# Interleaving the dense work of a 512-token chunk, in pieces of up to four matmuls, with the attention forward of the next chunk

## The chip, the cores and the metric

The kernel runs on one core of one Trainium2 chip. The metric is device microseconds (us) from the first to the last instruction of that core, as a median of several runs. PE is the matmul engine, DVE the vector engine, ACT the scalar engine (which computes the exponentials here and also issues 8 DMAs in the kernel before), POOL the GpSimd engine, SP the engine that issues most DMAs here (1161 of 1266 in the kernel before). "PE clock" is the granted clock of PE as a share of full speed, as the profile records it.

## The reference

It is one transformer block with adaptive layer norm, forward and backward: S = 2048 tokens, D = 512, 32 heads of 16, an MLP 512 → 1792 → 512 with squared ReLU, all in bf16. The kernel returns the output and nine gradients. Cut to what matters:

```python
def block(x, wqkv, wo, w1, b1, w2, b2, c, w_mod):
    sa, ca, ga, sb, cb, gb = split(silu(c) @ w_mod, 6)
    h = layernorm(x) * (1 + ca) + sa
    x = x + ga * (attention(h, wqkv, heads=32) @ wo)       # softmax attention
    h = layernorm(x) * (1 + cb) + sb
    r = relu(h @ w1 + b1)
    return x + gb * (r * r @ w2 + b2)

def reference(inputs, grad_out):
    out, vjp = jax.vjp(block, *inputs)
    return out, *vjp(grad_out)
```

## The kernel before

It runs in stages, one after the other: preparation (layer norm, Q, K, V), attention forward, the dense stage (projection, MLP forward and MLP backward, for each of four 512-token chunks), the weight gradients of the dense layers, the attention backward, and the rest. The first two of the following pieces are what the change weaves together.

The attention forward is a loop over units. A unit is one 128-key tile against 512 queries for a group of four heads. It has four score matmuls, two exponentials of 128x1024 elements on ACT, and, two units later, four PV matmuls. All of these matmuls use only a quarter of the array each (32 rows or 32 columns, placed by `tile_position`; the trace names them 32\*128 and 128\*32, and the dense ones 128\*128).

```python
psS = pool("psS", bufs=3, PSUM)     # score tiles of two banks each
psO = pool("psO", bufs=2, PSUM)     # accumulators of PV
# ... cut: fload brings the K and Q tiles of a group of heads ...
def fscore(u):
    ET = ework.tile([P, 4, 512], BF, name="ET")
    for pair in range(2):
        ps = psS.tile([P, 2, 512], F32, name="psST")
        for hi in range(2):
            r = 32 * (2 * pair + hi)
            PE.matmul(ps[:, hi, :], kt_sb[r:r + 32, kt * P:(kt + 1) * P], qt_sb[r:r + 32, :],
                      start=True, stop=True, tile_position=(r, 0))
        ACT.activation(ET[:, 2 * pair:2 * pair + 2, :], ps[:], AF.Exp, scale=SCALE)
# ... cut: fpv: four PV matmuls into oacc; after 16 key tiles oacc is evicted ...

# build of the padded, transposed QKV weights for the last stage, beside the forward:
for t3 in range(3):
    for hg in range(HG):
        # ... cut: every second hg loads a transposed tile tmpT ...
        for hq in range(4):
            POOL.dma_start(out=wT_bld[o0:o0 + DH, ...], in_=tmpT[r0:r0 + DH, :])   # 96 in all
POOL.dma_start(out=wT_st[:], in_=wT_bld[:])

for u in range(NF + 6):             # NF = 512 units
    if u < NF: fscore(u)
    if 2 <= u < NF + 2: fpv(u - 2)
    if fdone ...: ffinish(...)      # normalise a finished chunk, store it in o_st
```

Only then comes the dense stage, with all weights resident in both orientations and seven PSUM banks:

```python
psm = pool("psM", bufs=7, PSUM)
def dense_chunk(c):
    # ... cut: loads; a = O @ wo, layer norm, then ...
    for fc in range(FC):                                  # 14 blocks of the MLP
        pz = mm()                                         # one PSUM bank
        for ic in range(DC):                              # four matmuls 128x128x512
            PE.matmul(pz[:], w1_nat[:, ic, fc * P:(fc + 1) * P], h2T[:, ic, :], ...)
        # ... eviction with ReLU on ACT or DVE; square on DVE ...
    # ... cut: r*r @ w2, the same two products backward, dOs = da @ wo^T ...
for c in range(QC):
    for _ in dense_chunk(c): pass
```

The weight-gradient stage loads activations and gradients back from DRAM (gf_g, O_g, da_g, h_g and the tokens of the MLP, 22 MB in all; the first ten loads, 19 MB, are issued before any result is written) and runs 544 matmuls (the trace has records of 538) into eight banks of PSUM, with evictions alternating between ACT and DVE:

```python
for key, src in (("gf", gf_st), ("O", o_st), ("da", da_st), ("h2", h2_st)):
    SP.dma_start(out=toks[key][:], in_=src[:])
# ... cut: loads of s and dz ...
for oc in range(DC):
    acc = psg.tile([P, 512], F32, name="aw")              # bufs=8
    for t in range(TT): PE.matmul(acc[:], toks["O"][...], toks["da"][...], ...)
    if oc % 2 == 0: ACT.activation(wblk, acc, AF.Identity)
    else:           DVE.tensor_copy(wblk, acc)
# ... cut: the same for the gradients of w2 and w1 ...
```

Of the kernel before, what the change touches and what calls it, by code (L numbers as in the profile page):

```python
# [17 lines left out]
BF = dt.bfloat16  # L18
# [16 lines left out]
def kernel(  # L35
# [46 lines left out]
    dOs_tok = persist.tile([P, TT, D], BF, name="dOs_tok")  # L82
# [7 lines left out]
    o_st = dram.tile([P, TT, D], BF, name="o_st")  # L90
    da_st = dram.tile([P, TT, D], BF, name="da_st")
# [188 lines left out]
    with ExitStack() as ph:  # L280
        wk = ph.enter_context(tc.tile_pool(name="phC", bufs=2))
        ework = ph.enter_context(tc.tile_pool(name="phCe", bufs=4))
        psS = ph.enter_context(tc.tile_pool(name="psS", bufs=3, space=bass.MemoryType.PSUM))
        psO = ph.enter_context(tc.tile_pool(name="psO", bufs=2, space=bass.MemoryType.PSUM))
# [3 lines left out]
        fh, fe, fcur = {}, {}, {}  # L288
# [8 lines left out]
        def fscore(u):  # L297
            qc, hg, kt = funits[u]
            qt_sb, kt_sb = fh[qc, hg]
            ET = ework.tile([P, 4, 512], BF, name="ET", tag="ET")  # L300
            fe[u] = ET
            for pair in range(2):
                ps = psS.tile([P, 2, 512], F32, name="psST", tag="psST")
                for hi in range(2):
                    r = 32 * (2 * pair + hi)
                    PE.matmul(ps[:, hi, :], kt_sb[r:r + 32, kt * P:(kt + 1) * P], qt_sb[r:r + 32, :],  # L306
                              start=True, stop=True, tile_position=(r, 0))
                ACT.activation(ET[:, 2 * pair:2 * pair + 2, :], ps[:], AF.Exp, scale=SCALE)  # L308

        def fpv(u):  # L310
            qc, hg, kt = funits[u]
            if kt == 0:
                fcur["o"] = psO.tile([P, 512], F32, name="oacc", tag="oacc")
                if hg == 0:
                    fcur["rr"] = wk.tile([H, 512], F32, name="rrows", tag="rrows")
                    fcur["ou"] = wk.tile([P, 4, HG, P], BF, name="O_un", tag="O_un")
# [19 lines left out]
        fdone = []  # L336

        def ffinish(qc, rr, ou):
            O_c = wk.tile([P, 4, D], BF, name="O_c", tag="O_c")
            for ti in range(4):  # L340
                t = qc * 4 + ti
                pr = psO.tile([P, 512], F32, name="prinv", tag="oacc")
# [6 lines left out]
            SP.dma_start(out=o_st[:, qc * 4:(qc + 1) * 4, :], in_=O_c[:])  # L349

        NF = len(funits)
        fload(0, 0)
        wtp = ph.enter_context(tc.tile_pool(name="phW", bufs=1))
        wT_bld = wtp.tile([P, 16, D], BF, name="wT_bld")
        POOL.memset(wT_bld[:], 0.0)
        for t3 in range(3):
            for hg in range(HG):
                if hg % 2 == 0:
                    tmpT = wtp.tile([P, D], BF, name="tmpT", tag="tmpT", bufs=2)
                    SP.dma_start(out=tmpT[:], in_=A_wqkv[:, (t3 * 4 + hg // 2) * P:(t3 * 4 + hg // 2 + 1) * P], transpose=True)  # L360
                for hq in range(4):
                    r0 = (hg % 2) * 64 + hq * DH
                    o0 = 32 * hq + (DH if t3 == 1 else 0)
                    POOL.dma_start(out=wT_bld[o0:o0 + DH, (0 if t3 == 0 else 8) + hg, :], in_=tmpT[r0:r0 + DH, :])
        POOL.dma_start(out=wT_st[:], in_=wT_bld[:])
        with tc.manual_schedule(engines={PE.engine, ACT.engine}):
            for u in range(NF + 6):
                if u < NF:
                    if funits[u][2] == 4 and u + TT < NF:
                        fload(*funits[u + TT][0:2])  # L370
                    fscore(u)
                if 2 <= u < NF + 2:
                    fpv(u - 2)
                if fdone and (u - 2 >= fdone[0][0] or u == NF + 5):
                    ffinish(*fdone.pop(0)[1:])

    vaugpool.release()



    with ExitStack() as ph:
        ffw = ph.enter_context(tc.tile_pool(name="ffw", bufs=1))
        wk = ph.enter_context(tc.tile_pool(name="phM", bufs=2))
        cb = ph.enter_context(tc.tile_pool(name="phMc", bufs=1))
        psm = ph.enter_context(tc.tile_pool(name="psM", bufs=7, space=bass.MemoryType.PSUM))
        psr = ph.enter_context(tc.tile_pool(name="psMr", bufs=1, space=bass.MemoryType.PSUM))
        wo_nat = ffw.tile([P, DC, D], BF, name="wo_nat")
        SP.dma_start(out=wo_nat[:], in_=A_wo.rearrange("(oc p) j -> p oc j", p=P))
        w1_nat = ffw.tile([P, DC, FF], BF, name="w1_nat")
        SP.dma_start(out=w1_nat[:], in_=B_w1.rearrange("(ic p) f -> p ic f", p=P))  # L390
        w2_nat = ffw.tile([P, FC, D], BF, name="w2_nat")
        SP.dma_start(out=w2_nat[:], in_=B_w2.rearrange("(fc p) d -> p fc d", p=P))
        b2row = ffw.tile([1, D], BF, name="b2row")
        SP.dma_start(out=b2row[:], in_=B_b2.rearrange("(o f) -> o f", o=1))
        w1T = ffw.tile([P, FC, D], BF, name="w1T")
        w2T = ffw.tile([P, DC, FF], BF, name="w2T")
        woT = ffw.tile([P, DC, D], BF, name="woT")
        for oc in range(DC):
            SP.dma_start(out=w2T[:, oc, :], in_=B_w2[:, oc * P:(oc + 1) * P], transpose=True)
        for fc in range(FC):  # L400
            SP.dma_start(out=w1T[:, fc, :], in_=B_w1[:, fc * P:(fc + 1) * P], transpose=True)
        for oc in range(DC):
            SP.dma_start(out=woT[:, oc, :], in_=A_wo[:, oc * P:(oc + 1) * P], transpose=True)
        prow = psr.tile([P, 512], F32, name="prow")

        def rowsum(j, src, t):
            PE.matmul(prow[32 * j:32 * j + 1, :], ones_bf[:, 0:1], src, start=(t == 0), stop=(t == TT - 1),
                      tile_position=(0, 32 * j), skip_group_check=True)

        def mm():  # L410
            return psm.tile([P, 512], F32, name="pm", tag="pm")

        def t4():
            return cb.tile([P, 4, DC, P], BF, name="T4", tag="T4", bufs=2)

        def flat(x):
            return x.rearrange("p a b -> p (a b)")

        def dense_chunk(c):
            ts = slice(4 * c, 4 * c + 4)  # L420
            O_c = cb.tile([P, 4, D], BF, name="O_m", tag="O_m")
            SP.dma_start(out=O_c[:], in_=o_st[:, ts, :])
            x0_c = cb.tile([P, 4, D], BF, name="x0_c", tag="x0_c")
            SP.dma_start(out=x0_c[:], in_=x_dram[:, ts, :])
            g_c = cb.tile([P, 4, D], BF, name="g_c", tag="g_c")
            SP.dma_start(out=g_c[:], in_=g_dram[:, ts, :])
            OT = t4()
            SP.dma_start(out=OT.rearrange("p t o q -> p (t o) q"), in_=flat(O_c), transpose=True)
            gf_c = cb.tile([P, 4, D], BF, name="gf_c", tag="gf_c")
            DVE.tensor_tensor(gf_c[:], g_c[:], gb_bc.unsqueeze(1).to_broadcast([P, 4, D]), ALU.mult)  # L430
            SP.dma_start(out=gf_st[:, ts, :], in_=gf_c[:])
            gfT = cb.tile([P, 4, DC, P], BF, name="gfT", tag="gfT")
            SP.dma_start(out=gfT.rearrange("p t o q -> p (t o) q"), in_=flat(gf_c), transpose=True)
            x1_c = cb.tile([P, 4, D], BF, name="x1_c", tag="x1_c")
            a_c = cb.tile([P, 4, D], BF, name="a_c", tag="a_c")
            xn2_c = cb.tile([P, 4, D], BF, name="xn2_c", tag="xn2_c")
            mv4 = wk.tile([P, 4, 2], F32, name="mv4", tag="mv4")
            for ti in range(4):
                pa = mm()
                for oc in range(DC):  # L440
                    PE.matmul(pa[:], OT[:, ti, oc, :], wo_nat[:, oc, :], start=(oc == 0), stop=(oc == DC - 1))  # L441
                ACT.activation(a_c[:, ti, :], pa[:], AF.Identity)  # L442
                tmp = wk.tile([P, D], BF, name="atmp", tag="atmp")
                DVE.tensor_tensor(tmp[:], a_c[:, ti, :], ga_bc, ALU.mult)
                DVE.tensor_tensor(x1_c[:, ti, :], tmp[:], x0_c[:, ti, :], ALU.add)
                st6 = wk.tile([P, 6], F32, name="st6", tag="st6")
                DVE.bn_stats(st6[:], x1_c[:, ti, :])
                DVE.bn_aggr(mv4[:, ti, :], st6[:])
            sd4 = wk.tile([P, 4], F32, name="sd4", tag="sd4")
            DVE.tensor_scalar(sd4[:], mv4[:, :, 1], EPS, None, ALU.add)  # L450
            ACT.activation(sd4[:], sd4[:], AF.Sqrt)
            DVE.reciprocal(rstd2[:, ts], sd4[:])
            for ti in range(4):
                t = 4 * c + ti
                DVE.tensor_scalar(xn2_c[:, ti, :], x1_c[:, ti, :], mv4[:, ti, 0:1], rstd2[:, t:t + 1], ALU.subtract, ALU.mult)
# [527 lines left out]
```

## Time and profile before

The time is 3627.5 us (median of four fast runs, 3620.1 to 3629.0); the profiled execution spans 3621.8 us. The stages, from windows of the trace:

| stage | from – to, us | length | what limits it |
|---|---|---|---|
| preparation | 0 – 287 | 287 | PE and DVE |
| attention forward | 287 – 1236 | 949 | ACT, 940 us busy |
| dense stage | 1236 – 1727 | 491 | nothing is full: PE 276 us busy, DVE 253 |
| weight gradients | 1727 – 1858 | 131 | PE, 113 us |
| start of backward | 1858 – 1871 | 13 | DMA |
| attention backward | 1871 – 3307 | 1436 | PE, DVE and ACT together |
| rest | 3307 – 3622 | 315 | not touched |

The head of the page, its busy line, and three rows of the picture of 40 slices (each digit is a slice of 90.5 us; 9 means busy for 90% or more; PEclk is the clock in tenths):

```profile
span 3621.8 us, 47309 instructions
...
PE 2861.2 (79%) x17554; PEld 811.5 (22%) x17605; DVE 1861.7 (51%) x2725; ACT 2166.0 (60%) x3501; POOL 338.4 (9%) x390
...
PE   3688999999999665556778888888888888886746
...
ACT  0008999999999600000037777878777877784202
...
PEclk7985555555555577778888887888878878897967
```

The row of ACT is full (9) from slice 5 to slice 13 and then falls to 0: that is the forward followed by the dense stage. PE shows 9 in the same slices, but its clock is 5 there, half speed. The two stages need different engines and stand one after the other: this is what the change wants to use.

The windows view of the kernel before gives the same by stage. Its columns are the stretch and its length, then busy time and number of instructions of PE, PE weight loads, DVE, ACT and POOL, then the clock, the share of the DMA engines and GB/s:

```profile
core 0: us, PE busy (x) PEld busy (x) DVE busy (x) ACT busy (x) POOL busy (x), PEclk, DMA share, GB/s
287.00:1236.00 949.00, 870.28 (x4108) 163.69 (x4108) 33.42 (x56) 940.37 (x1025) 64.33 (x126) 0.50 0.12 34
1236.00:1727.00 491.00, 275.93 (x1089) 107.17 (x1108) 253.40 (x590) 30.90 (x49) 88.13 (x101) 0.76 0.62 147
1727.00:1858.00 131.00, 112.68 (x538) 53.74 (x544) 10.10 (x17) 9.65 (x17) 0.50 (x1) 0.92 0.51 205
1858.00:1871.00 13.00, 0.15 (x3) 0.14 (x4) 2.58 (x2) 1.35 (x2) 3.04 (x2) 0.62 0.98 348
1871.00:3307.00 1436.00, 1243.17 (x10224) 340.84 (x10220) 1188.81 (x1024) 1119.97 (x2206) 142.37 (x103) 0.84 1.15 204
```

The group of the exponentials, with busy time, mean length in ns, and the idle time of ACT just before them and what ended most of it:

```profile
L308 ACT ACTIVATE ET<-psST 128x1024 bf16<-128x1024 f32 x1024 | 939.1, 1697 | 5.9 <-PE psST L306 5.9
```

ACT was idle for only 5.9 us before 1024 exponentials: ACT sets the pace of the forward, 0.917 us for each, 1.83 us for a unit. A unit in the timeline (start, length, engine, operation; `x4` joins four matmuls):

```profile
801.82 0.62 PE L322 MATMUL oacc<-ET,vaug 128*32 128x512 bf16 x4
...
802.37 1.35 PE L306 MATMUL psST<-qt_sb,kt_sb 32*128 32x512 bf16 x4
...
803.65 0.62 PE L322 MATMUL oacc<-ET,vaug 128*32 128x512 bf16 x4
```

Four score matmuls are spread over 1.35 us and four PV matmuls over 0.62 us, so that PE counts as busy for nearly the whole of 1.83 us. But it streams only about 3 x 0.427 = 1.28 us of that (an estimate: the four PV matmuls start within 0.01 us of each other and the four score matmuls in two pairs, 0.74 us apart, which I count as three streams; 427 ns is the spacing that matmuls of this width have at half clock in the first burst of the dense stage, 1301.9 to 1304.5 us).

### The profile page before, as it was taken

The page shows a single profiled execution, that of the slowest core. Times are in us where ns is not written, and L with a number is a line of the kernel's source. Part 1 is how long each engine was busy: PE and PEld are TensorE (multiplying, and loading weights), DVE is VectorE, ACT ScalarE, POOL GpSimd, SP SyncE. Part 2 cuts the span into 40 slices and gives each one's busy share as a digit, 9 for nine tenths or more (in the row PEclk, how much of TensorE's full clock was granted, in tenths as well). Part 3 has the DMA queues.
Part 4 walks back from the last instruction along what each step waited for, and adds up shares of the span by engine and source line. Part 5 has one row for each costly group of instructions (what it writes and reads, how often), then busy time and mean ns, then how long its engine had stood idle before and what let it go on. Part 6 is the DMA issues. An engine that isn't in the chain of part 4 may idle for free.

```text
span 3621.8 us, 47309 instructions
## 1 busy us (share of the span) xinstructions
PE 2861.2 (79%) x17554; PEld 811.5 (22%) x17605; DVE 1861.7 (51%) x2725; ACT 2166.0 (60%) x3501; POOL 338.4 (9%) x390
## 2 busy tenths in 40 slices
PE   3688999999999665556778888888888888886746
PEld 1231111111111122222332222222222222221312
DVE  8860000000000145555038787888788878884781
ACT  0008999999999600000037777878777877784202
POOL 2006000000000012121000101010101010000000
PEclk7985555555555577778888887888878878897967
DMA  3123010010011355566669999999999999999112
GB/s 122 60 112 108 27 33 27 27 33 27 27 33 33 95 142 141 137 159 116 264 166 199 211 200 212 200 212 200 210 199 214 195 214 197 205 198 207 64 64 88
DMA packets 1331989, 487.18 MB, mean 135 GB/s; under 512 B 1275299, under 2 KB 1307559, under 8 KB 1328557
## 3 DMA queue, kind: packets, MB, share of 16 engines
q1 hardware_dynamic: 1312030, 478.38, 63.0%
q10 hardware_dynamic: 16512, 2.10, 0.4%
q0 software_dynamic: 3216, 3.68, 0.4%
q8 instruction: 139, 2.28, 0.2%
q14 instruction: 92, 0.75, 0.1%
HBM read 101.28 MB, written 71.98 MB: 48 GB/s over the span
## 4 chain that ended last, share of the span: by engine, by line
PE 24%; DMA 17%; DVE 5%; ACT 5%; issue 3%; SPq 1%; POOL 0%; DVEq 0%; POOLq 0%; ACTq 0%
DMA dsT<-dS_u 14%; PE psS_u L686 6%; PE dqacc L738 4%; ACT E_u L688 4%; PE accVK L723 3%; PE accVK L714 2%; PE psS_x L686 2%; DVE dS_u L700 2%; PE aw L619 1%; SPq L910 1%; PE aw L628 1%; DVE dqkv_tok L814 1%; PE psD_u L698 1%; DVE dh1acc L822 1%; DMA iqs<-q_st 1%
## 5 line engine op out<-in xcount | busy, mean ns | idle before, releaser
L700 DVE TENSOR_TENSOR dS_u<-psD_u,E_u 128x1024 bf16<-128x1024 f32 x1024 | 1188.8, 1218 | 248.7 <-PE psD_u L698 166.5
L688 ACT ACTIVATE E_u<-psS_u 128x512 bf16<-128x512 f32 x1536 | 867.0, 633 | 298.6 <-PE psD_u L698 274.0
L308 ACT ACTIVATE ET<-psST 128x1024 bf16<-128x1024 f32 x1024 | 939.1, 1697 | 5.9 <-PE psST L306 5.9
L306 PE MATMUL psST<-qt_sb,kt_sb 32*128 32x512 bf16 x2048 | 620.4, 597 | 81.3 <-DMA qt_sb<-QtP 10.0
L686 PE MATMUL psS_u<-ik,iq 32*128 32x512 bf16 x1536 | 523.3, 437 | 22.4 <-DMA ik<-KtP 13.4
L326 DVE COPY ostage<-oacc 128x512 f32<-128x512 f32 x32 | 22.1, 692 | 897.4 <-PE oacc L322 897.4
L698 PE MATMUL psD_u<-iv,ido 32*128 32x512 bf16 x2048 | 450.8, 435 | 15.9 <-DVE dS_u L700 9.4
L738 PE MATMUL dqacc<-dsT,KS_tok 128*32 128x512 bf16 x2048 | 213.1, 504 | 157.9 <-DMA dsT<-dS_u 131.7
L688 ACT ACTIVATE E_u<-psS_x 128x512 bf16<-128x512 f32 x512 | 332.6, 650 | 3.2 <-PE psD_u L698 1.9
L322 PE MATMUL oacc<-ET,vaug 128*32 128x512 bf16 x2048 | 317.0, 609 | 0.6 <-ACT ET L308 0.6
L306 PEld LDWEIGHTS <-kt_sb 32*128 32x128 bf16 x2048 | 104.8, 99 | 561.4 <-issue 561.4
L723 PE MATMUL accVK<-E_u,dOs_tok 128*16 128x512 bf16 x2048 | 227.8, 435 | 0.0
L686 PE MATMUL psS_x<-ik,iq 32*128 32x512 bf16 x512 | 211.8, 414 | 0.5
L686 PEld LDWEIGHTS <-iq 32*128 32x128 bf16 x2048 | 99.3, 93 | 374.9 <-issue 374.4
L698 PEld LDWEIGHTS <-ido 32*128 32x128 bf16 x2048 | 123.7, 93 | 223.9 <-issue 199.5
L442 ACT ACTIVATE a_c<-pm 128x512 bf16<-128x512 f32 x16 | 9.6, 597 | 260.7 <-PE pm L441 260.7
L753 POOL TENSOR_TENSOR dQacc<-dQacc,dqtmp 128x512 f32<-128x512 f32 x64 | 81.1, 1267 | 849.1 <-ACT dqtmp L748 849.1
L472 PE MATMUL pm<-h2T,w_nat 128*128 128x512 bf16 x218 | 58.0, 432 | 81.0 <-DVE h2T L460 80.4
L714 PE MATMUL accVK<-dS_u,qz_12477 128*32 128x512 bf16 x1024 | 114.4, 437 | 9.2 <-ACT vkb L726 6.8
L714 PE MATMUL accVK<-dS_u,qz_12478 128*32 128x512 bf16 x1024 | 111.3, 423 | 6.4 <-ACT vkb L726 5.6
L266 PE MATMUL ppad<-xn1T,wpadT 128*128 128x512 bf16 x376 | 98.6, 407 | 21.8 <-DVE stagep L269 16.2
L322 PEld LDWEIGHTS <-vaug 128*32 128x32 bf16 x2048 | 57.3, 102 | 224.6 <-issue 224.6
(1034 smaller groups left out, 2375.8 us busy)
## 6 DMA issues: line engine op xcount, KB each, us to landing
kt_sb<-KtP SPq DMA_DIRECT2D x32, 512.0 KB
dsT<-dS_u SPq DMA_TRANSPOSE x512
stok_st<-s_tok SPq DMA_DIRECT2D x4, 1792.0 KB
dztok_st<-dz_tok SPq DMA_DIRECT2D x4, 1792.0 KB
QtP<-stagep SPq DMA_DIRECT2D x8, 512.0 KB
KtP<-stagep SPq DMA_DIRECT2D x8, 512.0 KB
VtP<-stagep SPq DMA_DIRECT2D x8, 512.0 KB
qt_sb<-QtP SPq DMA_DIRECT2D x32, 128.0 KB
```

The costliest lines, as they stand in the source:

```text
L266: PE.matmul(pp[:], wpadT[:, ic, which, hg, :], h1T[:, ic, qc * 512:(qc + 1) * 512], start=(ic == 0), stop=(ic == DC - 1))
L306: PE.matmul(ps[:, hi, :], kt_sb[r:r + 32, kt * P:(kt + 1) * P], qt_sb[r:r + 32, :], start=True, stop=True, tile_position=(r, 0))
L308: ACT.activation(ET[:, 2 * pair:2 * pair + 2, :], ps[:], AF.Exp, scale=SCALE)
L322: PE.matmul(oacc[32 * hq:32 * hq + 32, :], lhsT, ET[:, hq, :], start=(kt == 0), stop=(kt == TT - 1), tile_position=(0, 32 * hq), skip_grou ...
L686: PE.matmul(psS[:], st["q"][r:r + 32, qt * P:(qt + 1) * P], st["k"][r:r + 32, kc * 512:kc * 512 + 512], start=True, stop=True, tile_positi ...
L688: ACT.activation(bst[u][0][:, hq, :], psS[:], AF.Exp, scale=SCALE)
L698: PE.matmul(psD[:, hi, :], st["do"][r:r + 32, qt * P:(qt + 1) * P], st["v"][r:r + 32, kc * 512:kc * 512 + 512], start=True, stop=True, til ...
L700: DVE.tensor_tensor(dS_u[:, 2 * pair:2 * pair + 2, :], psD[:], E_u[:, 2 * pair:2 * pair + 2, :], ALU.mult)
L714: PE.matmul(cur["vk"][32 * hq:32 * hq + 32, :], hst[hg]["qz"][:, qt, hq, :], bst[u][1][:, hq, :], start=(qt == 0), stop=False, tile_positi ...
L723: PE.matmul(acc[32 * hq:32 * hq + DH, :], dOs_tok[:, qt, (hg * 4 + hq) * DH:(hg * 4 + hq + 1) * DH], E_u[:, hq, :], start=False, stop=(qt ...
L738: PE.matmul(acc[32 * hq:32 * hq + 32, :], KS_tok[:, kc * 4 + kt, h * DH:h * DH + 32], tT[:, :, hq * 4 + kt, :], start=(kt == 0), stop=(kt ...
L753: POOL.tensor_tensor(dst2, dst, tmp[:], ALU.add)
```

## The change

The intent: while ACT computes the exponentials of chunk c + 1, PE and DVE do the dense work of chunk c. Only the last chunk's dense work stays exposed. `dense_chunk` becomes a generator that yields after each piece of up to four matmuls; a number yielded is a count of units to wait, for transposes through DMA. The loop takes one piece per unit. The diff, cut to its core:

```diff
-        psS = ... bufs=3 ; psO = ... bufs=2          # 8 banks in all
+        pools["s"]  = ... bufs=3    # score tiles, six banks
+        pools["o"]  = ... bufs=1    # PV accumulator, one bank
+        pools["mm"] = ... bufs=1    # dense pieces, one bank (8 for the last chunk)
 for u in range(NF + 6):
     if u < NF: fscore(u)
     if 2 <= u < NF + 2: fpv(u - 2)
+    if dense:
+        if wait > 0:
+            wait -= 1
+        else:
+            wait = next(dense[0], -1)
+            ...
     if fdone ...: ffinish(...)      # now ends with dense.append(dense_chunk(qc, O_c, qc == QC - 1))
+for _ in vaug_left: pass             # the dense work of the last chunk

 def dense_chunk(c, O_c, act):        # act: evictions on ACT only for the last chunk
+    w1_nat = load_wA(False); w2_nat = load_wB(False)    # weights now share two buffers:
+    ...; w2T = load_wA(True); ...; w1T = load_wB(True)  # reloaded in each chunk and orientation
-    DVE.tensor_tensor(gf_c[:], g_c[:], gb_bc..., ALU.mult)
+    POOL.tensor_tensor(gf_c[:], g_c[:], gb_bc..., ALU.mult)
+    yield 6
     for fc in range(FC):
         # four matmuls, eviction
+        yield 0
     # ...
+    yield 8                          # after the transpose daT, before dOs
-    rowsum: a matmul with ones into a PSUM bank of its own
+    rowsum: an addition on POOL into SBUF
-    dOs_tok stays in SBUF
+    dOs_c is stored to dOs_st; dOs_tok is loaded again before the backward
-    # wT build beside the forward, 96 small DMAs issued by POOL
 # weight-gradient stage, after the big loads have been issued:
+    ACT.dma_start(out=wT_bld[o0:o0 + DH, ...], in_=tmpT[r0:r0 + DH, :])   # the same 96
+    ACT.dma_start(out=wT_st[:], in_=wT_bld[:])
```

The change also transposes the MLP tokens in parts and writes dOtP in two halves per chunk.

## The prediction

> **What bounds the kernel now.** Windows by stage: preparation 0-287 us, attention forward 287-1236, dense stage 1236-1727 (to the first load of the weight-gradient stage), weight gradients to 1858, backward to 3307, rest to 3622. The forward is bound by ACT: 940 of 957 us busy, 1024 exponentials 0.917 us apart (1.83 us per unit of two), while DVE is busy 37 us, DMA 12%, and the granted PE clock is 0.50. The dense stage is serial and badly filled: four chunks of 140, 110, 109 and 118 us, each with some 69 us of PE, waiting on transposes and evictions.
>
> **What the change does.** Chunks 0-2 go into the forward: about 68 pieces of four matmuls, about 107 of 128 units per chunk.
>
> Saving: the exposed dense time (last PV to first gradient load) is 491 us now. For chunk 3 alone I expect 157: its first inputs are prefetched, but w2T and w1T are reloaded inside it (14 transposes took 18.5 us of SP, 4 took 13.7; about +15) and dOtP now takes 16 issues at 0.55 us. Saving 334 us.
>
> **Costs.**
> 1. PE in the forward: scores and PV now take about 3 x 0.43 us of stream time per unit at clock 0.5 (an estimate from the 427 ns spacing of cold matmuls in the dense stage). Four dense matmuls add 1.71 us cold (3.0 > 1.83: PE-bound), 0.86 us warm (1.5 < 1.83: hidden). [...]the dense bursts go from 427 ns to 215 ns after some 3 us, and the backward runs at 0.84. So I expect the clock to rise in dense stretches.
> 2. One PSUM bank for dense pieces: eviction 0.69-0.75 us against about 1 us before the next piece: nearly hidden. One oacc bank, ffinish through one bank, Sqrt on ACT with two table loads of 1.28 us per chunk, and daT waiting behind a weight load: together with 1, 15 us per chunk, 45 in all.
> 3. The wT build (96 small DMAs, 12 transposes; 60 us now, on POOL at 0.49 us each, hidden) moves into the weight-gradient stage, issued by ACT. In the built order 80 of these issues stand ahead of the second eviction of ACT, and their transposes stand behind 19 MB of loads (now 50 us). With eight banks, PE runs on for six groups and then stalls: I expect +45 us there.
> 4. dOs_tok is reloaded (2 MB) before the backward: +8 us.
>
> Sum: 3628 - 334 + 45 + 45 + 8 + about 8 of small ends = 3400 us.
>
> **Predicted:** 3400 us, 8 in 10 between 3325 and 3510. Faster by over 2%: 0.95; within 2%: 0.03; slower: 0.02.
>
> **What would show the steps right or wrong.** Forward about 1000 us long with ACT still over 93% busy and PE clock over 0.65 in the dense stretches (windows). Exposed dense stage about 157 us, with PE waits on w2T and w1T. In the weight-gradient stage, 30-60 us of PE idle with ACT held by wT_bld issues (timeline, waits): stage about 175 us against 131.
>
> **What would make it wrong.** The clock staying near 0.5 in mixed units: up to 68 x 1.2 us per chunk, +240 us in all. DVE or SP order holding PE at the single bank or at a kt_sb load: a lengthened forward with ACT idle on psST.

## The result

After the change the median is 3386.1 us (four fast runs, 3378.3 to 3388.1). The ratio to before is 0.933, with a 95% interval of 0.931 to 0.935. Here and below a ratio is the mean time of one kernel's fast runs over that of the other's of the same rounds, so it is not quite the ratio of the medians quoted. The profiled execution spans 3386.2 us. The same views as before, for the kernel after; first the page:

```profile
span 3386.2 us, 47396 instructions
...
PE 2663.9 (79%) x17485; PEld 788.3 (23%) x17549; DVE 1932.1 (57%) x2770; ACT 2157.3 (64%) x3474; POOL 372.3 (11%) x345
...
PE   2778998888888885348697889898898978885746
...
ACT  0006999999999992000586878787787868784202
...
PEclk7986555975975976778788878888878889897867
```

ACT is still at 9 through the forward, now with PE clocks of 9 and 7 mixed with 5. The slices after it show no long stretch without ACT beyond the last chunk's dense work and the weight gradients. The stages, in the windows view (dense work of the last chunk 1280 to 1427, weight gradients to 1616):

```profile
287.00:1280.00 993.00, 876.23 (x4861) 216.96 (x4888) 276.51 (x530) 955.10 (x1034) 148.58 (x146) 0.70 0.41 103
1280.00:1427.00 147.00, 71.83 (x267) 28.48 (x272) 79.09 (x161) 8.69 (x13) 39.54 (x39) 0.73 0.65 125
1427.00:1616.00 189.00, 115.81 (x538) 54.47 (x544) 9.84 (x16) 9.40 (x17) 6.83 (x2) 0.79 0.47 169
1616.00:1635.00 19.00, 0.26 (x3) 0.14 (x4) 2.84 (x3) 1.60 (x2) 3.35 (x2) 0.63 0.97 362
1635.00:3072.00 1437.00, 1240.57 (x10218) 341.42 (x10215) 1189.34 (x1024) 1119.09 (x2206) 142.57 (x103) 0.84 1.15 204
```

| stage | before | after | difference | predicted |
|---|---|---|---|---|
| forward | 949 | 993 | +44 | +45 |
| dense work that is exposed | 491 | 147 | −344 | −334 |
| weight gradients | 131 | 189 | +58 | +45 |
| start of backward | 13 | 19 | +6 | +8 |
| backward and rest | 1751 | 1751 | 0 | +8 |
| sum | | | −236 | −228 |

The trace accounts for all of it: 3621.8 − 236 = 3386.

**The forward.** The group of exponentials after:

```profile
L523 ACT ACTIVATE ET<-psST 128x1024 bf16<-128x1024 f32 x1024 | 945.5, 1311 | 34.7 <-PE psST L521 34.5
```

ACT's idle time before the exponentials went from 5.9 to 34.7 us; the rest of the 44 us is other work on ACT (square roots and table loads) and slightly longer exponentials (945.5 us busy against 939.1). A unit in a dense stretch:

```profile
656.60 0.40 PE L521 MATMUL psST<-qt_sb,kt_sb 32*128 32x512 bf16 x4
656.77 0.69 DVE L423 SCALAR_TENSOR_TENSOR rT<-pm,rT 128x512 bf16<-128x512 f32 x1 [1.18 <-PE pm L420]
...
656.92 0.40 PE L537 MATMUL oacc<-ET,vaug 128*32 128x512 bf16 x4
657.39 0.08 DVE L423 DVE_READ_ACCUMULATOR rT<-pm,rT 128x1 f32 x1
...
657.52 1.02 PE L420 MATMUL pm<-gfT,wA 128*128 128x512 bf16 x4 [0.20 <-DVE rT L423]
...
658.48 0.40 PE L521 MATMUL psST<-qt_sb,kt_sb 32*128 32x512 bf16 x4
```

The four score matmuls now take 0.40 us instead of 1.35. Not all of this is the clock: before, the second pair is held back by about 0.7 us, and four that stand together at half clock take 0.61 us in this trace (at 724.65). The four dense matmuls take 1.02. The clock is 0.93 in the window 582 to 640 and 0.97 from 640 to 700. It falls back to 0.50 in the pauses between dense phases (745 to 790). The unit takes 658.48 − 656.60 = 1.88 us, against 1.83 before. What sets 1.88 is the single dense bank. Its matmuls wait 0.20 us for the DVE eviction that ends at 657.47, which takes 0.69 + 0.08 us and itself waits for the matmuls before.

Each chunk costs the forward 14.7 us more (44 over three chunks). In the first of the three, ACT waits 10.3 us for scores, in ten waits; six of them are of 0.7 to 1 us, each beside one of the first pieces after a pause, which still run at the cold clock (1.87 to 1.89 us for the four matmuls, as at 585.29, 588.21 and 675.98). The unit of 1.88 us holds for the product shown: over a longer stretch, from 590.5 us on, 54 exponentials are 0.92 us apart on average, so 0.05 us a unit is the most that the single bank costs. Another part is the square root of the layer norm on ACT, with a table load before it (563.82) and another before the next exponential (565.34), of 1.28 us each, and 1.16 us of idle time before them. The largest single stall is this one, in the timeline of the phase after the wait for daT:

```profile
726.35 4.05 POOL L336 TENSOR_TENSOR gf_c<-g_c,modbc 128x2048 bf16<-128x2048 bf16 x1
...
726.67 3.83 DVE L489 TENSOR_SCALAR dOp<-delta 128x32 bf16<-128x32 f32 x1
...
730.36 0.68 DVE L482 TENSOR_TENSOR dOs_c<-pm,r_inv 128x512 bf16<-128x512 f32 x1
...
731.09 1.87 PE L478 MATMUL pm<-woT,daT 128*128 128x512 bf16 x4 [3.31 <-DVE dOs_c L482]
...
732.25 0.24 DVE L489 TENSOR_SCALAR dOp<-delta 128x32 bf16<-128x32 f32 x1
...
733.60 1.94 ACT L523 ACTIVATE ET<-psST 128x1024 bf16<-128x1024 f32 x2 [4.11 <-PE psST L521]
```

The DVE instruction at 726.67 writes 128x32 elements and takes 3.83 us, where the same instruction at 732.25 takes 0.24 us. POOL is executing a multiplication (gf_c of the next chunk, which the change moved from DVE to POOL) from 726.35 to 730.40, and the DVE instruction ends 0.10 us after it. The eviction of the dense bank stands behind it (730.36), PE waits 3.31 us for that, and ACT runs out of scores for 4.11 us. The same happens once in each of the three chunks (726.67, 978.47 and 1229.50). I call this the collision. The trace shows a coincidence: POOL issued 0.32 us earlier, and the DVE instruction lasted as long as POOL's did. What holds the DVE instruction up is not shown; that POOL's multiplication does it is my reading of these records, and the runs below bear on it only indirectly. The multiplication itself takes 4.05 us on POOL (128x2048 in bf16), where it took 1.23 us on DVE in the kernel before. The same coincidence is older than the change: in three of the four chunks of the kernel before, one of the four tensor_scalar instructions that make h2T takes 4.03 to 4.07 us instead of 0.40, beside POOL's multiplication of h_c that began 0.13 to 0.16 us earlier. It comes back in the exposed chunk after the change (4.02 us).

**The weight gradients.** This is the one place where the change added a visible hole. ACT's and PE's timelines there (ACTq is ACT's DMA issuing):

```profile
1454.77 0.60 ACT L641 ACTIVATE wblk<-aw 128x512 bf16<-128x512 f32 x1 [125.21 <-PE aw L648]
1483.41 52.40 ACTq L636 DMA_DIRECT2D wT_bld<-tmpT  x80
1535.90 0.60 ACT L641 ACTIVATE wblk<-aw 128x512 bf16<-128x512 f32 x1 [80.54 <-DMA wT_bld<-tmpT]
```

```profile
1484.79 1.03 PE L655 MATMUL aw<-gf_g,s_11851 128*128 128x512 bf16 x4
1536.55 1.87 PE L655 MATMUL aw<-gf_g,s_11845 128*128 128x512 bf16 x4 [50.74 <-ACT wblk L641]
```

ACT issues 80 small copies in a row from 1483.41, for 52.4 us, and its second eviction (1535.90) stands behind them in its instruction stream. The eight PSUM banks of the stage fill up and PE stands still for 50.74 us. These 80 come so late because they wait for ten of the 12 transposes on SP, which stand behind the big loads (SP issues the ten from 1451.93 to 1527.85). A second, smaller loss is that da_g, which the first matmuls need, is issued 13 us after O_g, so that PE starts 22.2 us after the first load of the stage, instead of 17.7 before:

```profile
1427.05 0.41 SPq L619 DMA_DIRECT2D O_g<-o_st  x1
1440.38 0.32 SPq L619 DMA_DIRECT2D da_g<-da_st  x1
```

It does not wait for the last chunk's da, whose store was issued at 1396.03. The trace puts 12.9 us of SP's wait there down to the first copies of the wT build. In both runs below that take the copies from ACT, da_g follows O_g within 0.5 us. Why SP waits for these copies, the trace does not show.

**The exposed dense work** is 147 us. In the trace of this stretch PE waits 20.7 us for daT, 13.8 for h2T, 6.9 for OT, and only 6.9 us for the reloaded w2T and w1T. Of the wait for h2T, 4.0 us are the collision of DVE and POOL just described.

### The profile page after: what moved, and what is told of

Same layout as the page of the kernel before. It is cut to its first block, busy times and chain, and to the rows that moved or that the text cites. A ratio compares the mean times of both kernels' runs of the same rounds, so it can differ in the third digit from the quotient of the medians.

```text
span 3386.2 us, 47396 instructions
## 1 busy us (share of the span) xinstructions
PE 2663.9 (79%) x17485; PEld 788.3 (23%) x17549; DVE 1932.1 (57%) x2770; ACT 2157.3 (64%) x3474; POOL 372.3 (11%) x345
## 4 chain that ended last, share of the span: by engine, by line
PE 36%; DMA 21%; ACT 18%; DVE 12%; issue 6%; SPq 3%; ACTq 2%; POOL 0%; DVEq 0%; POOLq 0%
DMA dsT<-dS_u 16%; ACT ET L523 14%; PE psS_u L724 7%; PE dqacc L776 5%; ACT E_u L726 4%; PE accVK L761 3%; PE ppad L266 3%; PE accVK L752 2%; PE psST L521 2%; DVE dS_u L738 2%; PE psS_x L724 2%; PE pm L387 2%; ACTq L636 1%; PE pm L420 1%; PE pm L403 1%
## 5 line engine op out<-in xcount | busy, mean ns | idle before, releaser
L523 ACT ACTIVATE ET<-psST 128x1024 bf16<-128x1024 f32 x1024 | 945.5, 1311 | 34.7 <-PE psST L521 34.5
L521 PE MATMUL psST<-qt_sb,kt_sb 32*128 32x512 bf16 x2048 | 464.6, 507 | 85.2 <-ACT ET L523 37.7
L537 PE MATMUL oacc<-ET,vaug 128*32 128x512 bf16 x2048 | 270.4, 517 | 0.6 <-ACT ET L523 0.6
L521 PEld LDWEIGHTS <-kt_sb 32*128 32x128 bf16 x2048 | 91.4, 96 | 461.7 <-issue 456.8
L850 ACT ACTIVATE dqkv_tok<-ptq 128x64 bf16<-128x64 bf16 x128 | 28.6, 224 | 119.8 <-PE ptq L844 119.8
L776 PEld LDWEIGHTS <-KS_tok 128*32 128x32 bf16 x2048 | 52.1, 105 | 221.2 <-issue 179.0
```

The costliest lines, as they stand in the source:

```text
L537: PE.matmul(oacc[32 * hq:32 * hq + 32, :], lhsT, ET[:, hq, :], start=(kt == 0), stop=(kt == TT - 1), tile_position=(0, 32 * hq), skip_grou ...
L776: PE.matmul(acc[32 * hq:32 * hq + 32, :], KS_tok[:, kc * 4 + kt, h * DH:h * DH + 32], tT[:, :, hq * 4 + kt, :], start=(kt == 0), stop=(kt ...
```

## The experiments

The theory: the forward was bound by ACT and the dense work hides under it, because PE's clock rises with the dense matmuls (0.93 to 0.97 in the dense stretches, against 0.50 before) and they come in pieces small enough for the three score buffers; what is given back lies in the weight-gradient stage (ACT's issues) and in small stalls of the forward. Rivals: the gain comes from the higher clock rather than from the overlap; or from the dense code being better in itself; or the single dense bank, or PE's capacity, is what costs the 44 us; or the grain does not matter.

All outputs are right. The kernel after was not timed again beside these runs; the kernel before was, and its medians (3624.6 to 3627.5) agree within 0.1%, so I compare times across the rounds.

### Is it the overlap? All dense work at once

```diff
-        wait = next(dense[0], -1)
-        ...
+        for _ in dense.pop(0): pass          # the whole chunk at one place, forward stands still
```

> Same program, but each dense chunk is run out in one go when its attention chunk is finished, so nothing is interleaved. If the gain is overlap, each of chunks 0-2 costs its serial time again (110 us and more, since it has one PSUM bank here): 3386 - 44 + 3 x 110 to 150 = 3670 to 3790, no faster than the kernel before. If the gain comes from the rewritten chunk (row sums on POOL, in-place tiles, partial transposes), it stays below 3550.

Measured: 3823.6 us in one look, beside 3626.1 for the kernel before in the same rounds. It is 437 us slower than after, above the range I had given. The weight-gradient stage starts at 1862.7 instead of 1426.6 us, so all of it is in the forward, about 145 us per chunk more than after. From first to last PV the forward takes 1420 us instead of 942 in the kernel before, so that a chunk of dense work costs 159 us there. So the generator's dense code is no better in itself. With a single bank and no overlap it is slower than the old dense stage (109 to 140 us per chunk). The gain is the overlap.

### Is it the clock? Dummy matmuls in the kernel before

Four matmuls 128x128x512 into a PSUM bank of their own, per unit, in the kernel before (PV has one accumulator instead of two, to make room); then eight.

```diff
     if 2 <= u < NF + 2: fpv(u - 2)
+    for i in range(4):                        # 8 in the second run
+        PE.matmul(dmy[:], dsrc[:, 0:P], dsrc[:], start=(i == 0), stop=(i == 3))
```

> The kernel BEFORE, with four 128x128x512 matmuls whose result nobody reads added to every forward unit (2048 in all; results stay correct). This is the PE load of the change alone, without its DVE, DMA and PSUM evictions. If the clock rises under the load, PE needs about 1.5 us of the 1.83 us unit: the forward stays within 15 us of 949 us, clock over 0.85, total within 1% of 3627. If the clock stays at 0.5, the unit takes about 3.0 us: forward about 1530, total about 4200.

> The same with eight matmuls per unit: 11 x 0.216 = 2.4 us of warm PE against 1.83 us of ACT. The forward should become PE-bound at about 1230 us (clock over 0.9) and ACT fall to some 77% busy; total about 3900. If the forward stays near 950, PE has more room than I count, and if it goes to 2500, the clock stays cold.

The windows view for 320 to 1200 us of the kernel before, with four dummies, and with eight, in this order:

```profile
320.00:1200.00 880.00, 810.18 (x3828) 152.46 (x3825) 32.54 (x54) 874.06 (x955) 37.54 (x70) 0.50 0.11 33
```

```profile
320.00:1200.00 880.00, 873.84 (x5699) 285.55 (x5697) 32.55 (x54) 869.00 (x949) 34.23 (x63) 0.99 0.12 33
```

```profile
320.00:1200.00 880.00, 875.77 (x5604) 317.63 (x5602) 23.07 (x38) 677.98 (x700) 32.65 (x63) 1.00 0.09 26
```

With four, the clock goes from 0.50 to 0.99, PE takes on some 1870 more matmuls, and the exponentials keep their pace (955 ACT instructions before, 949 with dummies). The time is 3629.0 us against 3624.6 before. So a warm clock alone buys nothing here, and four full-array matmuls per unit cost nothing in this run: the clock rises with them. With eight, PE is full at clock 1.00, ACT falls to 678 of 880 us, the forward takes 1288 us from first to last PV instead of 942, and the time is 3970.4. The capacity of a unit therefore lies between four and eight such matmuls, and the change's pieces of four fit into it. My estimate for eight was 1230 us; the unit takes 2.49 us in the trace at 800 us.

### Does the grain matter? Four pieces at a time

The same dense work at the same average rate, but up to four pieces after one unit and then three units without.

```diff
-        wait = next(dense[0], -1)
+        for _ in range(4):
+            wait = next(dense[0], -1)
+            if wait != 0: break
+        ...
+        elif wait == 0: wait = 3
```

> Four pieces are issued back to back, then three units without: same work, coarser. Three score banks cover about 1.8 us of exponentials; four pieces take 3.4 us warm plus evictions of the single bank (about 1 us each). If grain matters, ACT loses about 3 us per group, 17 groups x 3 chunks: +100 to +200 us. If ACT is hidden by the buffers anyhow, within 20 us of 3386.

Measured: 3666.1 us, 280 more than after, and 1.1% slower than before (ratio 1.011, 1.010 to 1.013): the whole gain over the kernel before is gone. I had expected 100 to 200. The timeline of one group of pieces:

```profile
705.55 1.89 PE L420 MATMUL pm<-gfT,wA 128*128 128x512 bf16 x4
...
708.30 1.87 PE L420 MATMUL pm<-gfT,wA 128*128 128x512 bf16 x4 [0.86 <-DVE rT L423]
...
711.03 1.87 PE L420 MATMUL pm<-gfT,wA 128*128 128x512 bf16 x4 [0.86 <-DVE rT L423]
...
713.75 1.86 PE L420 MATMUL pm<-gfT,wA 128*128 128x512 bf16 x4 [0.86 <-DVE rT L423]
...
716.26 7.44 ACT L523 ACTIVATE ET<-psST 128x1024 bf16<-128x1024 f32 x8 [9.10 <-PE psST L521]
```

Four pieces hold PE from 705.55 to 715.6, 10 us, and ACT, which has three score tiles in hand, runs dry for 9.10 us. Each piece takes 1.87 us, so the clock is cold. Between pieces PE waits 0.86 us for the eviction of the only bank. In the window 600 to 900 us the granted clock is 0.59, where it is 0.80 after. In this product the matmuls, bunched with such gaps, do not lift the clock: the last piece of the group, 8 us after the first, still takes 1.86 us. Over the forward, ACT's idle time before the exponentials rises by 288 us, in 57 waits of 5.7 us on average where I had counted 3:

```profile
L523 ACT ACTIVATE ET<-psST 128x1024 bf16<-128x1024 f32 x1024 | 945.1, 1318 | 322.6 <-PE psST L521 322.5
```

That the pieces take twice as long at the cold clock is a part of this; how large a part, the runs do not show.

The gaps come from the single bank, so a second run took three dense banks, paid for with one score tile:

```diff
-    pools["s"] bufs=3 ; pools["mm"] bufs=1
+    pools["s"] bufs=2 ; pools["mm"] bufs=3
```

> The coarse grain of the run before (four pieces in a row, 3666 us) with three dense banks and two score buffers. There the dense matmuls ran at clock 0.5 with 0.86 us waits for the eviction between pieces. If the waits on the single bank are what made coarse slow (and kept the clock down), the group shrinks from 10.7 us to about 4 to 5 and the time falls to 3480 to 3560. If coarse grain alone starves ACT, it stays over 3600.

Measured: 3615.3 us, 51 less than the coarse version. The groups shrink to 3.7 to 5.6 us, but ACT still idles 4 to 6 us at each. The clock is 0.68. So the banks explain a fifth of the 280 us, or somewhat more, since the run also lost one score tile. The coarse grain itself is the rest. This run changes two things at once; the next one shows, at the fine grain, what the score tile is worth against other banks.

### Are the banks well spent? Two and two and two

```diff
-    pools["s"] bufs=3 ; pools["o"] bufs=1 ; pools["mm"] bufs=1
+    pools["s"] bufs=2 ; pools["o"] bufs=2 ; pools["mm"] bufs=2
```

> The changed kernel with the eight PSUM banks dealt out as two score buffers of two banks, two for PV and two for the dense pieces (was 3 x 2, 1, 1). In the dense stretches the unit is 1.88 us, set by the round of the single dense bank (0.95 PE + 0.17 + 0.77 DVE), not by ACT's 1.83. If the single bank is what the forward pays for: a few us to 15 faster than 3386. If the third score buffer carries ACT over the dense piece of 1.0 us, its loss costs 0.1 to 0.3 us per unit: 20 to 60 us slower.

Measured: 3425.0 us, ratio to before 0.946 (0.944 to 0.948), 39 us slower than after. ACT's idle time before the exponentials rises from 34.5 to 58.0 us, and the time that it is busy with them from 945.5 to 966.4 us:

```profile
L523 ACT ACTIVATE ET<-psST 128x1024 bf16<-128x1024 f32 x1024 | 966.4, 1024 | 60.6 <-PE psST L521 58.0
```

The third score tile is worth more than second banks for the dense pieces and the accumulator. The run changes three pools at once, so it does not measure the single dense bank alone; it shows that a second one, paid for with a score tile, loses time.

### The hole in the weight-gradient stage: who issues the wT build

First only the issuing engine, from ACT to POOL, in the same place:

```diff
-    ACT.dma_start(out=wT_bld[...], in_=tmpT[...])
+    POOL.dma_start(out=wT_bld[...], in_=tmpT[...])
```

> The 96 small copies of the wT build are issued by POOL instead of ACT, still in the weight-gradient stage. If ACT's queue (80 issues ahead of its second eviction) is what stalls PE there, the 51 us stall goes and the time falls from 3386 to about 3338. If the cost is the 12 transposes or the copies on the DMA queues themselves, whoever issues them, it stays within 10 us of 3386.

Measured: 3330.2 us (3329.0 to 3333.1), ratio 0.918 (0.917 to 0.920), 56 us less than after. The stage takes 136 us and PE no longer stalls. One caution: in this build the order on SP changed too (the transposes stand between the output writes), so that ACT's queue and SP's order are not separated by this run.

Then the build is back in the forward, where the kernel before had it. I took its 16 KB per partition of SBUF (8192 elements in bf16) to be no longer free there, which no run shows, so POOL writes the pieces straight to DRAM, onto a field it has first zeroed with 16 writes:

```diff
+    for i in range(16): POOL.dma_start(out=wT_st[:, i, :], in_=zrow[:])
+    ...                 POOL.dma_start(out=wT_st[o0:o0 + DH, ...], in_=tmpT[r0:r0 + DH, :])
-    # the build in the weight-gradient stage
```

> The wT build goes back into the forward (POOL, straight to DRAM[...]). If the whole build is what lengthened the weight-gradient stage: that stage falls from 189 us back to about 135 and the total to about 3332; the forward should grow by less than 5 us. If the longer stage has another cause (reload of dOs, late da load), less than half of that comes back.

Measured: 3331.4 us (3327.4 to 3334.5), ratio 0.919 (0.917 to 0.920), the same as with POOL in place. The stage is 131 us, as in the kernel before, and the forward is longer by about 1 us. Both runs show the same thing from two sides, with the caution above: the build costs 55 us only when ACT issues it between its own evictions. The 55 us are the stall of 50.7 and the 4.5 us by which PE started later: in this last run PE starts 17.6 us after the first load again. The cost of one issue is not the reason, as the two groups show (min/median/max in ns); the first is after, on ACT's queue, the second before, on POOL:

```profile
L636 ACTq DMA_DIRECT2D wT_bld<-tmpT x96: 514/600/1634, 1433.7 to 1535.2; - x96
```

```profile
L364 POOL DMA_DIRECT2D wT_bld<-tmpT x96: 487/487/727, 285.4 to 343.4; - x96
```

600 ns and 487 ns are alike. What differs is what stands behind them in the same queue.

### The 44 us of the forward: the square root, and the wait before dOs

The square root of the layer norm on DVE, by three Newton steps from a constant of 20 (this start fits the variances of these inputs; it is a probe and no general replacement):

```diff
-    ACT.activation(sd4[:], sd4[:], AF.Sqrt); DVE.reciprocal(rstd2[:, ts], sd4[:])
+    DVE.memset(y4, 20.0)                      # y <- y * (1.5 - 0.5 * (var + eps) * y * y), three times
+    for _ in range(3): ...
```

> The Sqrt of the dense layer norm leaves ACT: three Newton steps on DVE from a start value that fits these inputs (a probe, not a general kernel). If the two table loads and the Sqrt (2.76 us, with up to 1.2 us of gap, per chunk) are part of the 44 us by which the forward grew, the forward, to the last PV, ends 8 to 12 us earlier than 1279.6. If ACT had slack there, under 3 us.

Measured: 3374.8 us in one look, 11 less than after. The time from the first to the last PV in the trace shrinks by 8.9 us, about 3 per chunk, which is the two table loads (2.56 us) and the square root.

Then the wait after the transpose daT, from 8 to 12 units. I believed that PE waited for daT there.

```diff
-            yield 8
+            yield 12
```

> The pause between the transposes of da and the matmuls that read them is 12 units instead of 8. In the trace ACT stood still 3.5 to 4.1 us there in each chunk. If that is PE waiting in order for daT, the forward ends 9 to 13 us earlier than 1279.6; if it is DVE that runs late, a longer pause changes under 4 us.

Measured: 3371.9 us in one look; the forward shrinks by 13.8 us, about 4.6 per chunk. The gain, 14 us, is above the spread of runs, but the reason I gave is not the one the trace shows: there was no wait for daT to remove. The group of the DVE instruction that was held up, in the kernel after and then with the longer wait (min/median/max in ns):

```profile
L489 DVE TENSOR_SCALAR dOp<-delta x16: 224/236/3832, 726.7 to 1408.7; 128x32 bf16<-128x32 f32 x16
```

```profile
L489 DVE TENSOR_SCALAR dOp<-delta x16: 222/237/242, 733.5 to 1394.9; 128x32 bf16<-128x32 f32 x16
```

The longest of the 16 is 242 ns now. The dense phase starts four units later, POOL's multiplication runs while DVE is idle, and the collision does not happen. In the run without the square root, where the wait is still 8, the longest is still 3827 ns. This fits the reading that POOL's multiplication holds the DVE instruction up; the direct test, to leave the multiplication on DVE, I did not run, so it is not proved that nothing else moved with the four units.

### Putting the parts together

The build in the forward, the Newton steps, and the wait of 12:

> Three together: wT build in the forward, no Sqrt on ACT in the dense chunks, pause of 12. If they add: 3330 - 9 - 11 = 3310, at least 12 us under 3330; if they cover the same waiting, 3318 to 3325.

Measured: 3304.3 us (3300.9 to 3310.6), ratio 0.912 (0.910 to 0.913): 82 us less than after and 322 less than before. The forward from first to last PV takes 961.3 us (941.6 before, 986.4 after). Of the 82 us, 55 are the wT build and 25 the forward. About 20 us of extra forward remain, with ACT idle 19.8 us before the exponentials. Without the Newton start that is fitted to these data one would lose about 9 of them.

Last, I tried to take back the 6 us at the start of the backward by loading dOs_tok after the first head instead of before:

```diff
-    SP.dma_start(out=dOs_tok[:], in_=dOs_st[:])     # before KS_tok and load_head(0)
     load_head(0)
+    SP.dma_start(out=dOs_tok[:], in_=dOs_st[:])
```

> The same with the reload of dOs placed behind the first loads of the backward. I charged 8 us to this reload; aw end to the first exponential of the backward is 19.4 us against 13.6 before. If the reload is in the way of the loads that start the backward: 4 to 8 us faster than the run before it. If not (KS_tok alone decides): within 3 us.

Measured: 3306.4 us (3303.4 to 3314.0), ratio 0.912 (0.911 to 0.914): no gain. The first exponentials of the backward start about 4 us earlier (14.6 us after the last weight-gradient matmul ends instead of 18.3). But the first accumulation matmuls start at the same time in both, 26 to 27 us after it, because they wait for another load (the Q slices) through POOL. The wait only moved.

## Why the prediction was right

The total was predicted as 3400 us and came out as 3386. The signs named beforehand came too: the forward took 993 us with ACT 96% busy, and PE stood idle for 50.7 us behind ACT's issues of wT_bld.

1. *"The forward is bound by ACT."* Right. ACT was busy for 940 of 949 us, and adding four matmuls per unit to the kernel before left its time unchanged (one look).
2. *"Four dense matmuls add ... 0.86 us warm (1.5 < 1.83: hidden) ... So I expect the clock to rise in dense stretches."* Right. The clock is 0.93 to 0.97 there, the four score matmuls take 0.40 instead of 1.35 us, and the unit 1.88 us instead of 1.83. The ground for it was the kernel before: in the first burst of its dense stage the spacing of the matmuls goes from 427 to 216 ns 3.3 us after the first one (1301.53 to 1304.88 us), and the windows view gives a clock of 0.50 from 1302 to 1304 and of 1.00 from 1306 to 1308. That it would also rise in the mixed units was an estimate; the run with four dummies shows it (0.50 to 0.99). How busy PE was did not tell the clock: PE counted as busy for 92% of the 949 us of the forward before at a clock of 0.50, and for 87% of the 1436 us of the attention backward at 0.84. Nor did the part of the array alone: the matmuls of both stages use a part of it (32 rows or 32 columns in the forward; 32 rows, or 32 or 16 columns in the backward). What the gaps between the matmuls do, these runs do not separate.
3. *"One PSUM bank for dense pieces ... nearly hidden."* Right, at most 0.05 us a unit; and a second bank for them and one for PV, taken from the scores, made the kernel 39 us slower.
4. *"15 us per chunk, 45 in all."* The size was right (44), in part by luck, since one cause on the list was wrong: in the forward, *"daT waiting behind a weight load"* does not hold PE. In its place a DVE instruction of 0.24 us takes 3.83 us beside a POOL multiplication, once per chunk, and starves ACT for 3.5 to 4.1 us. The square root is about 3 us per chunk. The other causes on the list were not measured singly. The multiplication's move to POOL stood in the diff; the prediction has no cost for the collision.
5. *"For chunk 3 alone I expect 157."* It was 147. The term that the trace shows as mis-sized is the reload of w2T and w1T: *"about +15"* against a wait of 6.9 us.
6. *"With eight banks, PE runs on for six groups and then stalls: I expect +45 us there."* The mechanism was right in detail (PE stalls 50.7 us for ACT's second eviction, behind 80 issues). The stall lies within the 30 to 60 us given, but as a term of the sum it was put at 45, and the stage grew by 58 us: besides the stall, the first matmuls start 4.5 us later because the load of da_g waits for the build's first copies, which I had not counted. The run with POOL as issuer brought back 56 us, the one with the build in the forward 55.
7. *"dOs_tok is reloaded: +8 us."* It was 6. *"About 8 of small ends"*: these did not appear; backward and rest are unchanged.

The errors of points 5 and 7 (−20 together) and of point 6 (+13) cancel in part, so the total is closer than some of its terms; that part is luck.

## What to carry to other kernels

When one stage saturates one engine and the next stage is serial on the others, put the second under the first, in pieces no longer than the slack that the saturated engine's buffers give it: here pieces of four matmuls ran in the dense stretches at a clock of 0.93 and above and cost at most 0.05 us a unit, while the same work in groups of up to sixteen matmuls lost all of the gain over the kernel before. Weighing buffers, protect the engine that bounds the stage: a third score tile was worth more than second banks for everything else (by 39 us). And look at what the moved work takes from its new place: small DMA issues in front of an engine's evictions cost 55 us, though each took only 0.6 us, and beside a multiplication of 4.05 us that was moved to POOL, a DVE instruction of 0.24 us took 3.83 us.
